# Linear attention feeding a gated MLP: zero products ahead of the first load, k loaded first, other buffers at the attention's end, and one head pair of the first batch divided on the chip

## The chip, the cores and the metric

The kernel runs on one core of a Trainium2 chip. The metric is device time in microseconds of one launch. Three runs of the kernel before took 1244.53, 1247.38 and 1248.22 us; the median is 1247.38 us.

The core has engines that each work through their own instruction list in order: TensorE (matrix products; PE in the profile, its weight loads PEld), VectorE (DVE), ScalarE (ACT), GpSimd (POOL), and SyncE (SP), which here issues the transfers between DRAM and the on-chip memory. [...]

## The reference

Attention has 8 batches, 8 heads, 576 tokens and 64 columns a head; its result, read as 4608 tokens of 512 columns, goes through a gated MLP.

```python
def phi(x):                                        # 64 -> 256 features
    proj = np.einsum('bhsd,df->bhsf', x, w_phi)    # w_phi: 64 x 128
    proj = proj - np.max(np.abs(proj), axis=-1, keepdims=True)
    return np.concatenate([np.exp(proj), np.exp(-proj)], axis=-1)
q_p, k_p = phi(q), phi(k)
kv  = einsum('bhsf,bhsd->bhfd', k_p, v);  z = sum(k_p, axis=2)
num = einsum('bhsf,bhfd->bhsd', q_p, kv)
den = einsum('bhsf,bhf->bhs', q_p, z)[..., None] + 1e-06
x = (num / den).transpose(0, 2, 1, 3).reshape(4608, 512)
out = ((x @ w_a) * (x @ w_b)) @ w_out              # 512 -> 1536 -> 512
```

Everything is float32. The weights of the MLP are float64 values handed over as 64-bit words, which the kernel decodes.

## The kernel before

**Attention** goes through 32 units, each a pair of heads of one batch. For one unit the k side loads k and v, forms the projection of k (tile `pk`, line 233, with the doubled weight matrix `wk32`), takes the largest absolute value on DVE (L247), subtracts it (L248), forms both exponentials on ACT (L256, L257) and accumulates `kvps` (L299). v carries a column of ones, so that row 64 of the result is the sum z. `k_finish` transposes that. The q side (`q_side`, one call per head) projects q (`pq`, L357), copies it (`p32`, L358), finds the maximum over partitions on POOL (`mb`, L361), subtracts it (L362), takes exponentials (L365, L366), multiplies with kv (`pn`, L381) and copies the 65 rows to `xn` (L382): 64 rows of numerators and one of denominators. `xn` has one buffer. Then `den` and `xun` are written to DRAM (L383, L384).

**The division** is done per pair by `reciprocals` (L392 on), through DRAM: the two denominator rows are read back in 128 partitions of 9 (`r`, L397), get eps and a reciprocal (L399, L400), are written (`rec`, L402), the numerators are read (`x32`, L404), the reciprocals are read broadcast over 64 partitions (`rb`, L407), multiplied (L409) and written as `xnorm` (L411). Each of these is one step of a generator.

**The MLP** runs in two passes over the hidden columns. Pass 0 has 12 blocks of 384 tokens (`moe_block`, products `pa` and `pb` at L609, outputs `po` at L632) and is interleaved with the attention; the first block needs only batch 0. Its x comes in four chunks of 128 columns, one from each head pair (`first_block_x`: `x_chunk` reads `xnorm` at L573, `x_make` splits it into two halves at L151 and L158). Pass 1 (`second_pass`, L696 and L744) comes after.

**Order.** Every generator's steps get a turn number (`attention_steps`): unit i starts at turn 5i for the first ones, a q side uses turns 0, 3, 4, 6 and 9 after that (3 later for the second head), the reciprocal steps of batch 0 the turns in `REC_TURNS0`, the x steps `X_TURNS`. The steps are traced in that order, and a planner that models time then orders each engine's list: work that it finds ready may be pulled ahead of work that is not, and loads go ahead as their buffers come free. `behind` keeps a reciprocal's transfers after the loads traced so far, and its DVE steps after the last traced subtraction L362.

**PSUM.** Up to the attention's end its products use four buffers with tag `att` (and one `kvacc`), the MLP three in `ps_moe`. Then the attention's pools close, and a pool `ps_late` with five buffers takes their banks; the last four blocks of pass 0 use it for `pa`, `pb` and `po`.

**Constants.** `attention_consts` loads w_phi twice on SP (L116), ahead of all other loads, and DVE builds from it, among others, the doubled matrix `wk32` (a memset at L122 and two copies at L125).

Of the kernel before, what the change touches and what calls it, by code (L numbers as in the profile page):

```python
# [10 lines left out]
F32 = mybir.dt.float32  # L11
# [3 lines left out]
ALU = mybir.AluOpType  # L15
# [17 lines left out]

REC_TURNS0, REC_TURNS, X_TURNS = (0, 1, 1, 1, 2, 2), (1, 3, 4, 5, 7, 8), (0, 1)
DECODE_TURN, BLOCK_LAG = 2, 1
PACE0, PACE, PACE0_UNTIL = 0.65, 0.75, 30


PLAIN_K, PLAIN_Q, PLAIN_KV, PLAIN_NUM = 9, 6, 11, 9

# [19 lines left out]
@with_exitstack  # L60
def tile_kernel(ctx, tc, qP, qD, km, kr, vm, vr, w_phi, w_a, w_b, w_out, out):

# [49 lines left out]

    def attention_consts(a1):
        w2 = a1.tile([P, F], F32, tag="rb", name="w2")
        for j in range(2):
            nc.sync.dma_start(w2[j * D : (j + 1) * D, :], w_phi)  # L116
        wh = a1.tile([P, F], F32R, name="wh")
        wl = a1.tile([P, F], F32R, name="wl")
        nc.vector.tensor_copy(wh, w2)
        nc.vector.tensor_tensor(wl, w2, wh, op=ALU.subtract)  # L120
        wk32 = a1.tile([P, 2, F], F32, tag="rk", name="wk32")
        nc.vector.memset(wk32, 0.0)  # L122
        for j in range(2):
            rows = slice(j * D, (j + 1) * D)
            nc.vector.tensor_copy(wk32[rows, j, :], w2[rows, :])  # L125
        wk2 = a1.tile([P, 2, F], F32R, name="wk2")
        nc.vector.memset(wk2.bitcast(F32), 0.0)
        nc.vector.tensor_copy(wk2[:, 0, :], wh)
        nc.vector.tensor_copy(wk2[:D, 1, :], wl[:D])
        ident = a1.tile([P, P], F32, name="ident")  # L130
        make_identity(nc, ident)
        rvz = []
        for i in range(2):
            t = a1.tile([P, 2, 2, D + 1], F32, name=f"rvz{i}")
            nc.vector.memset(t, 0.0)
            for r in range(2):
                nc.vector.memset(t[r * REST : (r + 1) * REST, r, :, D : D + 1], 1.0)
            rvz.append(t)
        vaug = []
        for i in range(2):  # L140
            t = a1.tile([P, NFULL, 2, D + 1], F32R, name=f"vaug{i}")
            nc.vector.memset(t[:, :, :, D : D + 1].bitcast(F32), 1.0)
            vaug.append(t)
        return w2, wh, wl, wk32, wk2, ident, rvz, vaug

# [186 lines left out]
    def q_side(b, pr, j, a1, a2, ps, consts, st):  # L332
# [41 lines left out]
        parts = [(s, kv_, e_) for kv_, e_ in products(st["kv", b, pr], es) for s in range(2)]  # L374
        xn = a2.tile([P, S], F32, tag="xn", bufs=1, name=f"xn_{u}")
        for i in range(2):
            tok = slice(i * HALF, (i + 1) * HALF)
            pn = ps.tile([P, 512], F32, tag="att", name=f"pn_{u}_{i}")
            for n_, (s, kv_, e_) in enumerate(parts):
                at = dict(start=(n_ == 0), stop=(n_ == len(parts) - 1))  # L380
                nc.tensor.matmul(pn[: D + 1, :HALF], kv_[:, 2 * j + s, :], e_[:, s, tok], **at)  # L381
            nc.scalar.copy(xn[: D + 1, tok], pn[: D + 1, :HALF])  # L382
        nc.sync.dma_start(den[b][h : h + 1], xn[D : D + 1])  # L383
        nc.sync.dma_start(xun[b][pr * P : (pr + 1) * P].rearrange("(d h) s -> d h s", h=2)[:, j], xn[:D])  # L384
        yield

# [27 lines left out]
    def attention_steps(pools, consts, st):  # L414
# [3 lines left out]
        def plan(unit, turns):  # L418
            for t in turns:
                stages.append((t, len(stages), unit))  # L420

        for i in range(B * NPAIR):
# [13 lines left out]
            rec_turns = REC_TURNS if b else REC_TURNS0  # L436
            plan(reciprocals(b, pr, pools[0]), [t0 + Q_STEP + Q_TURNS[-1] + t for t in rec_turns])
            if b == 0:
                plan(x_first, [t0 + Q_STEP + Q_TURNS[-1] + rec_turns[-1] + t for t in X_TURNS])
            if pr == NPAIR - 1:  # L440
                plan(b, [t0 + Q_STEP + Q_TURNS[-1] + rec_turns[-1]])
        stages.sort(key=lambda x: x[:2])
# [139 lines left out]
    def first_block_x():  # L582

        for c in range(NCC):
            x32 = x_chunk(0, 0, c, xpool, 2)
            yield
            x_make(0, 0, c, x32, xpool)
            yield

    def moe_block(p, j):  # L590
# [8 lines left out]
        for f in range(NFS[p]):  # L599
            u = f"{p}_{j}_{f}"  # L600
            pab = {}
            for nm in ("a", "b"):
                acc = psum.tile([P, T], F32, tag="moe", name=f"p{nm}_{u}")
                hi, lo = weights[(p, f, nm)]
                k = 0
                for cc in range(NCC):
                    xh, xl = xs[cc]
                    for w, x in ((hi, xh), (hi, xl), (lo, xh)):
                        nc.tensor.matmul(acc, w[:, cc * P : (cc + 1) * P], x, start=(k == 0), stop=(k == 3 * NCC - 1))  # L609
                        k += 1  # L610
                pab[nm] = acc
# [186 lines left out]

    away = {}
    weights, pools_moe, xpools, block_x, blocks, marks, loads = {}, [ps_moe], [xpool], {}, [0], [], []  # L800
    with ExitStack() as c:
        pools = attention_pools(c)
        consts = attention_consts(pools[0])
        work, tasks, due, st = deque(), {}, 0.0, {}
# [109 lines left out]
```

## Time and profile before

| What | Value |
|---|---|
| Median of three runs | 1247.38 us |
| The profiled execution | 1247.68 us |
| Its span | 1245.9 us |
| PE busy | 1212.7 us (97%) |
| DVE, ACT, POOL busy | 883.4, 726.5, 152.8 us |
| Mean granted PE clock | 0.993 |

The profile is of one execution, 1.8 us longer than its span, since something lies before the first and after the last instruction. The span's start is zero in every view. A timeline row is: start, duration, engine, line, operation, output<-inputs, shapes, count; in brackets how long that engine stood idle just before, and what released it. A row of the chain of waits is: start, duration, what the end of the program was waiting for then. A row of the table by stretches gives, for each stretch of time, the busy time of each engine with its number of instructions, the granted PE clock, the busy share of the DMA engines and the rate. One product of float32 operands makes two records on PE.

### The profile page before, as it was taken

The numbers are of one execution on the slowest core, as the hardware profiler recorded it, in microseconds if no ns is written. First come the engines' busy times: TensorE is split into PE (matmuls) and PEld (weight loads), VectorE is DVE, ScalarE is ACT, GpSimd is POOL, SyncE is SP. The second block draws the span as 40 slices with busy tenths as digits, with TensorE's granted clock in tenths as the row PEclk, the third lists the DMA queues.
The fourth block names the chain that finished last, engine by engine and source line by source line (L and its number), as shares of the span: only waits on it lengthen the run. The fifth ranks groups of instructions, "written<-read, shape, count | busy, mean of one in ns | idle before, by whom it ended". The sixth has DMA issues, their size and how long they took to land.

```text
span 1245.9 us, 20872 instructions
## 1 busy us (share of the span) xinstructions
PE 1212.7 (97%) x7724; PEld 1135.5 (91%) x7724; DVE 883.4 (71%) x1510; ACT 726.5 (58%) x1503; POOL 152.8 (12%) x70
## 2 busy tenths in 40 slices
PE   7898999999999999999999899999999999999998
PEld 5566888999999999999999899998999999999997
DVE  7967877988898988898887498655455455455443
ACT  5766777888878878878887355433232222222221
POOL 2331222122122121222122000000000000000000
PEclk9998999999999999999999999999999999999999
DMA  8776664554555454554443556982221231231121
GB/s 220 221 205 191 171 174 128 146 157 120 141 151 146 130 166 118 142 151 139 112 126 87 165 169 214 356 283 73 85 93 45 68 98 38 68 101 35 52 68 51
DMA packets 132101, 168.34 MB, mean 135 GB/s; under 512 B 41056, under 2 KB 77408, under 8 KB 132000
## 3 DMA queue, kind: packets, MB, share of 16 engines
q1 hardware_dynamic: 132000, 167.02, 45.5%
q8 instruction: 60, 0.98, 0.3%
q14 instruction: 41, 0.34, 0.1%
HBM read 119.49 MB, written 47.48 MB: 134 GB/s over the span
## 4 chain that ended last, share of the span: by engine, by line
PE 79%; DMA 10%; DVE 4%; ACT 3%; issue 2%; SPq 1%; POOL 0%; DVEq 0%; ACTq 0%
PE pab L696 20%; PE po L744 12%; PE pb L609 11%; PE pa L609 11%; PE po L632 9%; PE kvps L299 6%; PE pn L381 6%; PE pq L357 2%; PE pk L242 1%; DMA kept_wl_o<-wl_o 1%; DMA xnorm<-x 1%; DMA raw_a<-in_w_a 1%; DMA v<-in_vm 1%; DMA kept_wf_q_b_s<-wf_q_b_s 1%; DMA x<-xnorm 1%
## 5 line engine op out<-in xcount | busy, mean ns | idle before, releaser
L361 POOL PARTITION_ALL_REDUCE mb<-p x64 | 152.1, 2377 | 524.2 <-ACT p L358 416.1
L609 PE MATMUL pa<-xh,wh_a 128*128 128x384 f32 x288 | 100.0, 347 | 4.4 <-ACT xn L382 3.5
L151 ACT CAST hh<-h 128x384 fp32r<-128x384 f32 (+1 forms) x126 | 68.1, 560 | 59.7 <-DVE h L719 27.1
L609 PE MATMUL pa<-xl,wh_a 128*128 128x384 f32 x288 | 99.1, 344 | 0.0
L609 PE MATMUL pb<-xh,wh_b 128*128 128x384 f32 x288 | 98.8, 343 | 0.0
L609 PE MATMUL pa<-xh,wl_a 128*128 128x384 f32 x288 | 98.6, 342 | 0.0
L609 PE MATMUL pb<-xl,wh_b 128*128 128x384 f32 x288 | 98.3, 341 | 0.0
L609 PE MATMUL pb<-xh,wl_b 128*128 128x384 f32 x288 | 98.1, 341 | 0.0
L632 PE MATMUL po<-hl,wh_o 128*128 128x384 f32 x288 | 97.8, 341 | 0.0
L632 PE MATMUL po<-hh,wh_o 128*128 128x384 f32 x288 | 96.3, 342 | 0.7 <-ACT o L644 0.7
L632 PE MATMUL po<-hh,wl_o 128*128 128x384 f32 x288 | 97.0, 340 | 0.0
L158 DVE TENSOR_TENSOR hl<-h,hh 128x384 fp32r<-128x384 f32 (+1 forms) x126 | 76.0, 617 | 22.2 <-ACT hh L151 22.1
L158 DVE TENSOR_TENSOR qel<-qe,qeh 128x1152 fp32r<-128x1152 f32 x46 | 62.4, 1356 | 31.4 <-ACT qeh L151 29.2
L163 DVE TENSOR_TENSOR qs<-q,qs 64x576 fp32r<-64x576 f32 x52 | 63.4, 1220 | 25.0 <-ACT qs L151 22.5
L382 ACT COPY xn<-pn 65x288 f32<-65x288 f32 x128 | 48.9, 396 | 28.3 <-PE pn L381 16.6
L749 DVE TENSOR_TENSOR o<-po,o 128x512 f32<-128x512 f32 x36 | 24.1, 689 | 56.4 <-PE po L744 34.3
L609 PEld LDWEIGHTS pa<-xh,wh_a 128*128 128x128 f32 x288 | 54.7, 190 | 5.9 <-ACT xn L382 3.8
L256 ACT ACTIVATE ke<-kd 128x512 f32<-128x512 f32 x64 | 40.8, 637 | 29.4 <-DVE kd L248 28.9
L711 ACT COPY low<-pab 128x512 f32<-128x512 f32 x27 | 15.8, 586 | 71.3 <-PE pab L696 63.8
L744 PE MATMUL po<-hl,back_h 128*128 128x512 f32 x144 | 56.3, 391 | 0.0
L744 PE MATMUL po<-hh,back_l 128*128 128x512 f32 x144 | 56.2, 391 | 0.0
L632 PEld LDWEIGHTS po<-hh,wh_o 128*128 128x128 f32 x288 | 53.9, 188 | 1.6 <-ACT o L644 1.1
(268 smaller groups left out, 3843.2 us busy)
## 6 DMA issues: line engine op xcount, KB each, us to landing
q<-in_qD SPq DMA_DIRECT2D x52, 288.0 KB
k<-in_km SPq DMA_DIRECT2D x55, 256.0 KB
xun<-xn SPq DMA_DIRECT2D x64, 144.0 KB
x<-xun SPq DMA_DIRECT2D x32, 288.0 KB
rb<-rec SPq DMA_DIRECT2D x32, 288.0 KB
xnorm<-x SPq DMA_DIRECT2D x32, 288.0 KB
part<-o SPq DMA_DIRECT2D x48, 192.0 KB
o<-part SPq DMA_DIRECT2D x36, 256.0 KB
```

Of the source, the lines that this page charges most:

```text
L151: eng.copy(dst, src)
L158: eng_lo.tensor_tensor(lo, src, hi, op=ALU.subtract)
L163: eng_lo.tensor_tensor(hi_lo[D:], src[D:], hi_lo[D:], op=ALU.subtract)
L256: nc.scalar.activation(e[:, :, 0, :], d, AF.Exp)
L299: nc.tensor.matmul(st["kv_ps", b, pr][:width, j], v_[:, j, :width], e_[:, j], start=(left == NFULL and j == 0 and n_ == 0), stop=(left == ...
L361: nc.gpsimd.partition_all_reduce(mb, p32, P, bass_isa.ReduceOp.absmax)
L381: nc.tensor.matmul(pn[: D + 1, :HALF], kv_[:, 2 * j + s, :], e_[:, s, tok], **at)
L382: nc.scalar.copy(xn[: D + 1, tok], pn[: D + 1, :HALF])
L609: nc.tensor.matmul(acc, w[:, cc * P : (cc + 1) * P], x, start=(k == 0), stop=(k == 3 * NCC - 1))
L632: nc.tensor.matmul(accs[cc], w[:, cc * P : (cc + 1) * P], h, **at)
L696: nc.tensor.matmul(acc[to][:, i], w_, x_, skip_group_check=True, **at)
L744: nc.tensor.matmul(acc[cc], w[:, cc * P : (cc + 1) * P], h, **at)
```

## The change

Five things are done.

1. `w_two`, the doubled projection matrix with zeros (128x2x128), is prepared as an input and loaded straight into `wk32`; this load and the two of w_phi are issued from ACT instead of SP. So SP's first issue is k. The memset and copies at L122 and L125 go.
2. One half of `vaug` is set to zero by DVE, and five products of zeros, 192 columns wide, go to PE before everything else, into an `att` buffer that nothing reads.
3. Pair 3 of batch 0 (`DIRECT`) doesn't go through `reciprocals`. Its copy to `xn` adds eps to row 64 on the way (a bias column), and the new function `divide` takes the reciprocal of that one row of 576, spreads it over 64 partitions by a product with a row of ones, multiplies, and writes the chunk of the first block straight into its on-chip tile and all of x to `xnorm`.
4. The turns of batch 0 change: reciprocal steps from (0, 1, 1, 1, 2, 2) to (0, 2, 2, 3, 5, 5), x steps from (0, 1) to (1, 2) after them; for pair 3, (1, 2) after its last q step. The turn in which the first block is released stays the same.
5. The last head's `xn` uses the buffer `mb` instead of `xn`, and in every block of pass 0 the products of the first hidden slice use `ps_moe` instead of the late pool.

```diff
-REC_TURNS0, REC_TURNS, X_TURNS = (0, 1, 1, 1, 2, 2), (1, 3, 4, 5, 7, 8), (0, 1)
+REC_TURNS0, REC_TURNS, X_TURNS = (0, 2, 2, 3, 5, 5), (1, 3, 4, 5, 7, 8), (1, 2)
+WARM, WARM_TIMES = 192, 5
+DIRECT = (3,)
...
-    def attention_consts(a1):
+    def attention_consts(a1, ps):
+        wk32 = a1.tile([P, 2, F], F32, tag="rk", name="wk32")
+        nc.scalar.dma_start(wk32, w_two)
+        vaug = [a1.tile([P, NFULL, 2, D + 1], F32R, name=f"vaug{i}") for i in range(2)]
+        busy = vaug[1].rearrange("p c j d -> p (c j d)")[:, :WARM].bitcast(F32)
+        nc.vector.memset(busy, 0.0)
+        warm = ps.tile([P, WARM], F32, tag="att", name="warm")
+        for _ in range(WARM_TIMES):
+            nc.tensor.matmul(warm, busy[:, :P], busy, start=True, stop=True)
         w2 = a1.tile([P, F], F32, tag="rb", name="w2")
         for j in range(2):
-            nc.sync.dma_start(w2[j * D : (j + 1) * D, :], w_phi)
+            nc.scalar.dma_start(w2[j * D : (j + 1) * D, :], w_phi)
...
-        wk32 = a1.tile([P, 2, F], F32, tag="rk", name="wk32")
-        nc.vector.memset(wk32, 0.0)
-        for j in range(2):
-            rows = slice(j * D, (j + 1) * D)
-            nc.vector.tensor_copy(wk32[rows, j, :], w2[rows, :])
...
+        ones = a1.tile([P, 4 * (D + 1)], F32, tag="rvl", name="ones")
+        nc.vector.memset(ones[:, :D], 1.0)
+        eps = ones[: D + 1, D : D + 1]
+        nc.vector.memset(eps, 0.0)
+        nc.vector.memset(eps[D : D + 1], EPS)
...
-        xn = a2.tile([P, S], F32, tag="xn", bufs=1, name=f"xn_{u}")
+        direct = b * NPAIR + pr in DIRECT
+        xn = a2.tile([P, S], F32, tag="mb" if h + 1 == H and b + 1 == B else "xn", bufs=1, name=f"xn_{u}")
...
-            nc.scalar.copy(xn[: D + 1, tok], pn[: D + 1, :HALF])
+            if direct:
+                nc.scalar.activation(xn[: D + 1, tok], pn[: D + 1, :HALF], AF.Identity, bias=consts[7])
+            else:
+                nc.scalar.copy(xn[: D + 1, tok], pn[: D + 1, :HALF])
+        if direct:
+            yield from divide(b, pr, j, xn, ps, consts)
+            return
...
+    def divide(b, pr, j, xn, ps, consts):
+        u = f"{b}_{2 * pr + j}"
+        row = xn[D : D + 1]
+        nc.vector.reciprocal(row, row)
+        for i in range(2):
+            tok = slice(i * HALF, (i + 1) * HALF)
+            pr_ = ps.tile([P, 512], F32, tag="att", name=f"prec_{u}_{i}")
+            nc.tensor.matmul(pr_[:D, :HALF], consts[8][D : D + 1, :D], row[:, tok], start=True, stop=True)
+            nc.vector.tensor_tensor(xn[:D, tok], xn[:D, tok], pr_[:D, :HALF], op=ALU.mult)
+        if j == 0:
+            block_x32[pr] = xpool.tile([P, T1], F32, tag="x32", bufs=2, name=f"x32_0_0_{pr}")
+        nc.sync.dma_start(block_x32[pr].rearrange("(d h) s -> d h s", h=2)[:, j], xn[:D, :T1])
+        nc.sync.dma_start(xnorm[b][pr * P : (pr + 1) * P].rearrange("(d h) s -> d h s", h=2)[:, j], xn[:D])
+        yield
...
-            plan(reciprocals(b, pr, pools[0]), [t0 + Q_STEP + Q_TURNS[-1] + t for t in rec_turns])
+            if i not in DIRECT:
+                plan(reciprocals(b, pr, pools[0]),     [t0 + Q_STEP + Q_TURNS[-1] + t for t in rec_turns])
...
-            x32 = x_chunk(0, 0, c, xpool, 2)
+            x32 = block_x32.pop(c) if c in block_x32 else x_chunk(0, 0, c, xpool, 2)
...
-                acc = psum.tile([P, T], F32, tag="moe", name=f"p{nm}_{u}")
+                acc = (psum if f else ps_moe).tile([P, T], F32, tag="moe", name=f"p{nm}_{u}")
```

More of the change, by code (lines that the diff above doesn't have):

```diff
@@ L60, in tile_kernel @@
 @with_exitstack
-def tile_kernel(ctx, tc, qP, qD, km, kr, vm, vr, w_phi, w_a, w_b, w_out, out):
+def tile_kernel(ctx, tc, qP, qD, km, kr, vm, vr, w_phi, w_two, w_a, w_b, w_out, out):
     nc = tc.nc
@@ L138, in attention_consts @@
             rvz.append(t)
-        vaug = []
-        for i in range(2):
-            t = a1.tile([P, NFULL, 2, D + 1], F32R, name=f"vaug{i}")
+        for t in vaug:
             nc.vector.memset(t[:, :, :, D : D + 1].bitcast(F32), 1.0)
-            vaug.append(t)
-        return w2, wh, wl, wk32, wk2, ident, rvz, vaug
+        ones = a1.tile([P, 4 * (D + 1)], F32, tag="rvl", name="ones")
[3 more added lines that the diff above has]
+        nc.vector.memset(eps[D : D + 1], EPS)
+        return w2, wh, wl, wk32, wk2, ident, rvz, eps, ones, vaug
     def engine(step, b):
@@ L436, in attention_steps @@
             rec_turns = REC_TURNS if b else REC_TURNS0
-            plan(reciprocals(b, pr, pools[0]), [t0 + Q_STEP + Q_TURNS[-1] + t for t in rec_turns])
+            if i not in DIRECT:
+                plan(reciprocals(b, pr, pools[0]),     [t0 + Q_STEP + Q_TURNS[-1] + t for t in rec_turns])
             if b == 0:
-                plan(x_first, [t0 + Q_STEP + Q_TURNS[-1] + rec_turns[-1] + t for t in X_TURNS])
+                plan(x_first, [t0 + Q_STEP + Q_TURNS[-1] + (0 if i in DIRECT else rec_turns[-1]) + t for t in X_TURNS])
             if pr == NPAIR - 1:
-                plan(b, [t0 + Q_STEP + Q_TURNS[-1] + rec_turns[-1]])
+                plan(b, [t0 + Q_STEP + Q_TURNS[-1] + (X_TURNS[-1] if i in DIRECT else rec_turns[-1])])
         stages.sort(key=lambda x: x[:2])
@@ L799, in tile_kernel @@
     away = {}
+    block_x32 = {}
     weights, pools_moe, xpools, block_x, blocks, marks, loads = {}, [ps_moe], [xpool], {}, [0], [], []
@@ L802, in tile_kernel @@
         pools = attention_pools(c)
-        consts = attention_consts(pools[0])
+        consts = attention_consts(pools[0], pools[2])
         work, tasks, due, st = deque(), {}, 0.0, {}
@@ L898 @@
     vr = vr.reshape(B, H // 4, 2 * (S - n), 2, 2, D)
+    w_two = np.zeros((2, D, 2, w_phi.shape[1]), w_phi.dtype)
+    for j in range(2):
+        w_two[j, :, j] = w_phi
+    w_two = w_two.reshape(2 * D, 2, -1)
     arrays = {
-        "qP": qP, "qD": qD, "km": km, "kr": kr, "vm": vm, "vr": vr, "w_phi": np.ascontiguousarray(w_phi),
+        "qP": qP, "qD": qD, "km": km, "kr": kr, "vm": vm, "vr": vr, "w_phi": np.ascontiguousarray(w_phi), "w_two": w_two,
         "w_a": turned(moe_w_a).view(np.int64), "w_b": turned(moe_w_b).view(np.int64), "w_out": moe_w_out.view(np.int64),
```

## The prediction

> **What bounds the kernel now.** I read the engine totals first, then the table by stretches, and then the timeline and the chain of waits where that table shows PE idle.
>
> ```profile
> span 1245.9 us, 20872 instructions
> ...
> PE 1212.7 (97%) x7724; PEld 1135.5 (91%) x7724; DVE 883.4 (71%) x1510; ACT 726.5 (58%) x1503; POOL 152.8 (12%) x70
> ```
>
> PE is busy for all but 33.2 us (1245.9 - 1212.7). A change that leaves PE's work as it is can win at most these 33 us, and what busy time is lost to a low clock. So the question is which of the idle time each edit touches.
>
> ```profile
> 0.00:10.00 10.00, 4.89 (x12) 3.88 (x13) 4.92 (x22) 2.43 (x3) 0.68 (x6) 1.00 0.68 171
> 10.00:20.00 10.00, 8.64 (x39) 5.98 (x37) 6.09 (x13) 6.15 (x14) 2.38 (x2) 1.00 1.09 279
> 20.00:30.00 10.00, 8.01 (x38) 5.23 (x39) 9.83 (x17) 7.92 (x18) 4.29 (x2) 1.00 0.72 199
> ...
> 90.00:100.00 10.00, 7.27 (x32) 4.87 (x31) 4.63 (x10) 3.35 (x8) 2.14 (x1) 0.91 0.42 127
> 100.00:110.00 10.00, 8.41 (x27) 5.17 (x28) 8.26 (x17) 6.84 (x16) 2.50 (x1) 0.57 0.77 222
> ...
> 695.00:700.00 5.00, 2.52 (x17) 1.84 (x15) 2.12 (x2) 0.93 (x2) 0.00 (x0) 1.00 0.41 128
> 700.00:705.00 5.00, 3.33 (x12) 3.32 (x13) 0.28 (x2) 0.69 (x2) 0.00 (x0) 0.74 0.31 93
> ...
> 800.00:810.00 10.00, 10.00 (x58) 10.00 (x57) 8.40 (x19) 5.72 (x13) 0.00 (x0) 1.00 1.04 384
> ...
> 830.00:840.00 10.00, 9.54 (x79) 9.33 (x78) 8.35 (x19) 2.79 (x7) 0.00 (x0) 1.00 0.78 227
> 840.00:850.00 10.00, 8.68 (x62) 8.01 (x61) 6.88 (x15) 4.50 (x10) 0.00 (x0) 1.00 0.57 185
> ```
>
> The columns are PE, PEld, DVE, ACT and POOL busy, then clock, DMA share and GB/s. Three places lie under the edits. The start has 5.1 us idle in the first 10 us. The first block's wait at 90 to 110 has 2.73 + 1.59 = 4.3 us idle, and a clock of 0.91 and 0.57. The attention's end at 695 to 705 has 2.48 + 1.67 = 4.15 us idle and a clock of 0.74. These are the three terms of the sum.
>
> **The start (loads, zero products).**
>
> ```profile
> 0.72 1.22 SPq L116 DMA_DIRECT2D w<-in_w_phi  x2
> 1.99 0.58 SPq L172 DMA_DIRECT2D k<-in_km  x1
> 5.11 3.75 PE L233 MATMUL pk<-wk,k 128*128 128x256 f32 x8 [5.11 <-DMA k<-in_km]
> 18.84 0.76 DVE L362 TENSOR_TENSOR p<-p,mb 128x576 f32<-128x576 f32 x1 [1.88 <-POOL mb L361]
> 113.55 1.89 PE L299 MATMUL kvps<-ke,v 128*65 128x256 f32 x8
> ```
>
> ```profile
> 1.37 2.21 DMA w<-in_w_phi
> 6.27 6.20 DMA raw_a<-in_w_a
> ```
>
> The first two fences are from the timeline and the chain of waits. PE's first product waits for k, issued at 1.99 behind the two w_phi loads. With these off SP, k is issued at 0.72, 1.27 us sooner, and lands by 5.11 - 1.27 = 3.84. `wk32` now arrives by a 128 KB load issued from ACT near 0.7. No row has that size: the 32 KB one took 2.21 us, the 512 KB one 6.20 us in a crowd, so it lands between 2.9 and 6.9; I take about 4, nearer to the small one. In the bad end the first product is 1.8 us later than now.
>
> The eight records of 256 columns at 5.11 take 3.75 us, where the same width later takes 1.89: PE starts at half speed, whatever the clock column says. Five zero products are ten records of 192 columns, at the slow rate 10 x (192/256) x 3.75/8 = 3.5 us. They wait only for one small memset, so they run from about 1.1 to 4.6, and k finds PE free at 4.6 instead of 5.11. If PE is by then at full speed, the first eight records end at 4.6 + 1.9 = 6.5 instead of 8.86, a gain of 2.3; if not, 0.5. All eight slow records lasted 3.75 us, so 3.5 us of zeros should nearly do. [...]
>
> How much is passed on? The first DVE subtraction on the q side still stands at 18.84 behind POOL, whose first reduction no edit touches, and from 20 us on DVE is the full engine (9.83 of 10). DMA is full in 10 to 20 (1.09). So of 0.5 to 2.3 I book 1.0, with bounds from a loss of 1.8 to a gain of 2.3. The DVE work taken out (a memset, two copies) and put in (four small memsets) lies in idle time: DVE is busy 4.92 of the first 10 us. If that cover were gone it would be under 1 us either way. The `vaug` memset waits for the zero products, with the reduction of the first `pk` behind it, which comes later in any case.
>
> **The first block's wait (division on the chip, turns).**
>
> ```profile
> 86.62 2.44 DMA r<-den
> ...
> 89.61 3.10 DMA rec<-r
> ...
> 92.76 3.60 DMA rb<-rec
> ...
> 97.17 2.08 DMA xnorm<-x
> 99.28 3.64 DMA x<-xnorm
> ```
>
> ```profile
> 82.28 0.39 ACT L382 COPY xn<-pn 65x288 f32<-65x288 f32 x1
> 88.11 0.51 ACT L151 CAST xh<-x 128x384 fp32r<-128x384 f32 x1 [1.82 <-DMA x<-xnorm]
> 89.16 0.17 DVE L399 TENSOR_SCALAR r<-r 128x9 f32<-128x9 f32 x1 [4.33 <-DMA r<-den]
> 96.39 0.76 DVE L409 TENSOR_TENSOR x<-x,rb 128x576 f32<-128x576 f32 x1 [5.12 <-DMA rb<-rec]
> 97.85 0.78 PE L233 MATMUL pk_r<-wk,rk 128*128 128x256 f32 x2 [2.22 <-issue]
> 102.94 0.51 ACT L151 CAST xh<-x 128x384 fp32r<-128x384 f32 x1 [1.28 <-DMA x<-xnorm]
> 106.58 2.85 PE L299 MATMUL kvps<-ke,v 128*65 128x256 f32 x8
> ```
>
> Pair 3's numerators are copied at 82.28, and its chunk is cast at 102.94: 20 us, five DRAM trips of 2.1 to 3.6 us each. Two of them stop DVE in its order, for 4.33 and 5.12 us. Behind the second stands the subtraction L248 that frees a PSUM buffer, so PE's `pk_r` waits 2.22 us. After this gap the eight records of 256 columns take 2.85 us instead of 1.89: the clock has dropped. [...]
>
> Without this chain the idle 4.3 us go. The clock's cost is busy time times what is missing: 8.41 x 0.43 + 7.27 x 0.09 = 4.3 us. Together 8.6 us.
>
> What comes instead, for each of two heads: a reciprocal of a row of 576, two products of 64x288, two multiplications, two transfers. The nearest rows:
>
> ```profile
> L399 DVE TENSOR_SCALAR r<-r x32: 161/168/271, 42.1 to 704.7; 128x9 f32<-128x9 f32 x32
> ```
>
> ```profile
> L400 DVE RECIPROCAL r<-r x32: 201/206/217, 44.2 to 704.9; 128x9 f32<-128x9 f32 x32
> 76.57 2.10 PE L381 MATMUL pn<-qe,kvh 128*65 128x288 f32 x8
> ```
>
> Four products of 288 columns take 2.10 us, so the four new ones add 2.1 us to PE; nothing hides that. A multiplication of 576 takes 0.76 (L409). The reciprocal of 9 elements takes 0.206 us and the addition 0.168. If the 38 ns are only a longer pipe, 576 elements cost about what L409 costs, 0.76. If they are a price per element, it is 38/9 = 4.2 ns more, 0.76 + 2.4 = 3.2 us. If all 206 ns scale, 13.2 us. I take 0.8, since both 9-element rows are mostly a fixed cost. DVE has 4.33 + 5.12 = 9.45 us of waiting here to cover 2 x (0.8 + 0.8). So pair 3's chunk is ready at 82.7 + 0.8 + 1.1 + 0.8, plus a transfer. No row has one between two on-chip tiles; the DRAM ones above take 2.08 to 3.64 us, so that is 87.5 to 89 in place of 103.
>
> The other turns move pair 2's chain: its multiplication now stands behind one more subtraction L362, about 1 us, so its cast at 88.11 becomes about 89. Neither chunk then comes later than 95.6, where PE ran dry. The eps on the way is free, one copy for another; five transfers of SP's go and two stay as substitutes. `xn` is held longer, by a reciprocal, two products and two multiplications, some 3 us, under ACT's own idle time here (it works 3.35 of 10). If that is not cover enough, ACT's copies for pair 4 wait up to 3 us. The term is 8.6 - 2.1 = 6.5 us.
>
> **The attention's end (other buffers).**
>
> ```profile
> 695.76 0.48 ACT L644 COPY o<-po 128x384 f32<-128x384 f32 x1 [0.30 <-PE po L632]
> 700.93 0.69 ACT L382 COPY xn<-pn 65x288 f32<-65x288 f32 x2 [4.69 <-DMA xun<-xn]
> 701.67 0.44 PE L609 MATMUL pa<-xh,wh_a 128*128 128x384 f32 x1 [3.50 <-ACT xn L382]
> ```
>
> The last head's copy waits 4.69 us for the transfer that empties `xn`, and the next block's `pa` waits for that copy, since its PSUM bank is the attention's. `mb` is free by then, so the copy no longer waits; and `pa` no longer needs that bank: `ps_moe`'s last `po` was copied out at 695.76 + 0.48 = 696.24. PE's 3.50 us go, and with them the slow clock after them, 5 x (1 - 0.74) = 1.3 us. Later blocks have `ps_moe` standing free, at no cost. The term is 4.8 us; its bounds are 4.8 and 0, if another wait of the pool change takes over.
>
> **Sum.** 1.0 + 6.5 + 4.8 = 12.3 us, against the profiled execution: 1247.68 - 12.3 = 1235.4. The median of the runs is 0.3 lower, and I leave that inside the rounding: 1235.5 us. About 0.3%, 3.7 us, is what a measurement of this kernel can tell from no change.
>
> **The rivals.**
>
> *Slow reciprocal* (the other side). It sits in DVE's order, with the PE products and all of DVE's list behind it. At 3.2 us a row it adds 2 x 2.4 = 4.8, giving 1240; at 13.2 it adds 25 us, less at best the 9.45 of DVE's former waiting: 1251 to 1260. It turns the sign where 2 x (R - 0.8) eats 12.3 us, at R = 7 us or 12 ns an element. For it: the 206 against 168 ns. Against: at 4.2 ns an element more it stays far from 12. [...] Chance 0.10 that it costs over 2.4 us a row, half of that with a sign turned.
>
> *The late loads give it back.* After 800 the DMA engines are full (1.04) and PE idles 0.46 + 1.32 us at 830 to 850. If the loads that begin at the attention's end don't move with PE, the 4.8 us gained there come back as idle near 840: 1240.3. Against: up to 800 these loads are stepped by the blocks themselves, and their first issue hangs on the same last copy. Chance 0.15.
>
> *Pair 2 is late next.* If its chunk, two DRAM trips behind a later multiplication, comes 6 us after my 89, PE runs dry about as before, and half of the 6.5 is lost: 1238.7. For it: it has the turns moved back by three. Chance 0.10.
>
> *The zeros and the loads do nothing or harm*: 1236.4 to 1238.2, inside the forecast's own range, 1230 to 1238.5. The forecast has 0.60; 0.05 is left for a worse order by the planner, which I can't price, taken as losing most of the gain.
>
> The range is 1229.5 to 1243. Faster by over 0.3% holds the forecast, the milder slow reciprocal, and nearly all of the second and third rival, 0.89; within it, the planner's case and a remnant, 0.06; slower, the dear reciprocal, 0.05.
>
> **What would show it.** Right: the first `pk` near 4.6 with eight records in about 2 us; no DVE wait over 2 us between 80 and 105 and a clock of 1.00 there; `pa` within 0.5 us of the last `pn` near 690. Wrong: a RECIPROCAL row over 3 us; an `xh` cast after 97 that waits for `xnorm`; new idle at 820 to 850 of more than 1.8 us.

## The result and the profile after

The changed kernel takes 1257.65 us (median of four runs, 1252.54 to 1258.83) against 1246.24 us for the kernel before beside it. The ratio is 1.0079, 95% interval 1.0058 to 1.0099: slower, and outside the predicted range. A ratio here is an estimate from all the runs and not the quotient of the two medians, which is 1.0092. Two single slow runs further on, of 1291 us in e17 and 4219 us in e6, are left out of the ratios. The profiled execution took 1258.32 us. This page of the profile has its totals.

```profile
span 1256.5 us, 20911 instructions
...
PE 1219.1 (97%) x7742; PEld 1139.5 (91%) x7742; DVE 891.6 (71%) x1514; ACT 727.0 (58%) x1503; POOL 153.8 (12%) x70
```

PE is busy 6.4 us longer than before (1219.1 against 1212.7), about what the zero products and the products of the division take. It also idles 37.4 us instead of 33.2. So neither a gap nor busy time was saved on the whole. The table by stretches, with the columns of the one before, says where.

```profile
0.00:10.00 10.00, 7.97 (x29) 6.33 (x30) 4.73 (x24) 3.02 (x5) 0.68 (x6) 1.00 0.82 226
...
20.00:30.00 10.00, 7.77 (x26) 4.69 (x27) 9.79 (x17) 5.93 (x13) 4.50 (x2) 0.66 0.42 113
...
80.00:90.00 10.00, 8.03 (x37) 5.00 (x35) 6.99 (x9) 3.79 (x8) 0.34 (x1) 1.00 0.66 198
90.00:100.00 10.00, 6.80 (x21) 3.89 (x22) 6.54 (x7) 2.99 (x7) 1.80 (x1) 0.82 0.21 63
100.00:110.00 10.00, 10.00 (x41) 7.54 (x40) 5.31 (x11) 6.59 (x14) 2.14 (x1) 0.84 0.33 88
...
710.00:715.00 5.00, 1.71 (x9) 1.42 (x8) 1.78 (x3) 1.10 (x3) 0.00 (x0) 0.91 0.31 112
```

All three places still have their gap. From 20 to 30 us the clock is now 0.66. The first block's wait has moved from 90–110 to 80–100, with 5.2 us idle instead of 4.3, and a slow clock remains (0.82 and 0.84 where before has 0.91 and 0.57). The attention's end has 3.29 us idle in one piece. The timeline shows what stands in each place. First the start:

```profile
1.10 3.38 PE L123 MATMUL warm<-vaug 128*128 128x192 f32 x10 [1.10 <-DVE vaug L120]
4.53 1.99 PE L240 MATMUL pk<-wk,k 128*128 128x256 f32 x8
...
9.32 0.28 POOL masks.py:199 TENSOR_SCALAR_AFFINE_SELECT ident<-ident 128x128 f32<-128x128 f32 x1 [8.39 <-issue]
17.32 2.15 POOL L368 PARTITION_ALL_REDUCE mb<-p  x1 [7.72 <-issue]
...
22.23 0.67 PE L328 MATMUL pt<-ident,kvT 65*128 65x65 f32 x4 [4.71 <-ACT kvT L324]
22.69 6.28 PE L306 MATMUL kvps<-ke,v 128*65 128x256 f32 x16
```

The first products come as predicted (4.53, eight records in 1.99 us) and end 2.3 us ahead of before. POOL's first reduction does not come earlier: the five traces with the new start have it at 17.3 to 19.3 us, those with the old start and the identity matrix made on POOL at 15.1 to 18.9. PE runs dry at 22, for 4.71 us where before waited 2.93, and the sixteen records after the gap take 6.28 us instead of 2 x 1.89. Then the division:

```profile
79.23 3.74 DVE L405 RECIPROCAL xn<-xn 1x576 f32<-1x576 f32 x1
...
83.03 1.18 PE L409 MATMUL prec<-xn,ones 1*64 1x288 f32 x4 [1.21 <-DVE xn L405]
...
91.53 0.49 ACT L391 ACTIVATE xn<-pn,ones 65x288 f32<-65x288 f32 x1
...
92.05 3.74 DVE L405 RECIPROCAL xn<-xn 1x576 f32<-1x576 f32 x1 [3.43 <-ACT xn L391]
...
95.94 1.78 PE L409 MATMUL prec<-xn,ones 1*64 1x288 f32 x4 [2.10 <-DVE xn L405]
...
102.65 0.51 ACT L158 CAST xh<-x 128x384 fp32r<-128x384 f32 x1 [0.29 <-DMA x<-xn]
```

A reciprocal of one row takes 3.74 us, and PE, whose next product stands directly behind it, waits. The second head's numerators are complete only at 92.02, and pair 3's chunk is cast at 102.65, where the kernel before had it at 102.94. Last, the attention's end:

```profile
702.94 0.34 PE L640 MATMUL pa<-xh,wh_a 128*128 128x384 f32 x1
...
711.36 0.76 DVE L439 TENSOR_TENSOR x<-x,rb 128x576 f32<-128x576 f32 x1 [3.10 <-DMA rb<-rec]
712.03 0.55 DVE L645 TENSOR_TENSOR h<-pb,h 128x384 f32<-128x384 f32 x1
712.62 0.51 ACT L158 CAST hh<-h 128x384 fp32r<-128x384 f32 x1 [5.30 <-DVE h L645]
713.03 0.68 ACT L393 COPY xn<-pn 65x288 f32<-65x288 f32 x2
713.77 0.45 PE L640 MATMUL pa<-xh,wh_a 128*128 128x384 f32 x1 [3.29 <-ACT xn L393]
```

The copy no longer waits for its own buffer. It now stands on ACT behind a cast of a block, which waits for DVE's multiplication, which stands behind another that waits for `rb` from DRAM. And `pa` still waits for the copy: the block's first hidden slice, which has the experts' own pool, ran at 702.94 to 708.9, and the `pa` at 713.77 belongs to the second slice, whose pool still takes the attention's banks.

**A measure for where time is lost.** PE does the same products in all kernels, in somewhat different orders. For each trace I added up the work that PE had been given by each moment, without the zero products and those of the division. Each record counts with what it takes where nothing disturbs it, which the trace of before shows, from start to start, within 0.003 us: 0.216 us for 256 columns of the plain float32 products of the attention's first units and 0.243 for 288; in the later products 0.119, 0.132, 0.175 and 0.230 for 256, 288, 384 and 512 columns; 0.060 for a small transpose. A mere count of columns would shift the values by up to 2 us where orders differ, since a column of the early products takes nearly twice as long. The lag is the time at which a kernel has given PE as much as before had at the stated time, minus that time (us; negative is ahead). The times 210 and 690 lie clear of before's own gaps, near 199 and 700 us. A number in this table comes from the profiled execution alone.

| Kernel | 30 | 70 | 120 | 210 | 500 | 690 | 720 | 860 | 1200 |
|---|---|---|---|---|---|---|---|---|---|
| after | 2.9 | 5.3 | 7.7 | 9.3 | 10.4 | 9.0 | 7.9 | 8.5 | 8.5 |
| e1_start | 3.2 | 4.0 | 1.2 | 1.0 | 1.8 | 1.6 | 1.3 | -0.5 | -0.5 |
| e2_direct | -0.3 | -0.6 | 3.8 | 5.4 | 10.8 | 9.6 | 6.8 | 10.0 | 10.0 |
| e3_end | 1.3 | 1.4 | 1.1 | -0.4 | 0.9 | 1.3 | -4.3 | -6.4 | -6.4 |
| e4_copy | 4.0 | 7.3 | 2.7 | 5.8 | 7.0 | 5.6 | 5.0 | 5.5 | 5.5 |
| e9_turns | 3.1 | 1.9 | -1.9 | -4.9 | -3.6 | -4.2 | -5.5 | -4.0 | -4.0 |
| e11_mb | 1.1 | 0.5 | -1.0 | -0.9 | -0.7 | -0.2 | -4.8 | -3.9 | -3.9 |
| e12_later | 0.4 | 1.7 | -1.8 | -0.3 | 4.4 | 3.2 | 0.5 | 8.0 | 8.0 |
| e13_ready | 3.0 | 1.9 | -0.2 | 4.2 | 5.2 | 4.4 | 4.7 | 5.6 | 5.6 |
| e14_ready_mb | -0.3 | -0.9 | -1.9 | 2.6 | 3.7 | 3.2 | -1.4 | 1.8 | 1.8 |
| e15_turns_mb | 0.6 | -0.2 | -3.2 | -6.1 | -5.6 | -6.5 | -11.0 | -10.1 | -10.1 |
| e17_ready_only | 0.8 | -1.0 | -0.9 | -3.5 | -2.2 | -3.0 | -4.2 | -4.4 | -4.4 |
| e18_ready5 | 0.0 | 0.9 | -1.1 | 3.3 | 4.6 | 5.6 | 4.6 | 3.4 | 3.4 |

After loses 5.3 us by 70, 2.4 more by 120 and 1.6 more by 210, and gets 0.8 back from there to 1200. Its span is 10.6 us longer than before's; the other 2.1 us lie behind the last product. Of the 5.3, some 3 us can be chance: at 30 us the kernels with the old start lie anywhere from -0.3 to 3.1.

### The profile page after: what moved, and what is told of

It reads as the page before. It is cut to its first block, busy times and chain, and to the rows that moved or that the text cites. A ratio compares the mean times of both kernels' runs of the same rounds, so it can differ in the third digit from the quotient of the medians.

```text
span 1256.5 us, 20911 instructions
## 1 busy us (share of the span) xinstructions
PE 1219.1 (97%) x7742; PEld 1139.5 (91%) x7742; DVE 891.6 (71%) x1514; ACT 727.0 (58%) x1503; POOL 153.8 (12%) x70
## 4 chain that ended last, share of the span: by engine, by line
PE 70%; DVE 10%; DMA 9%; ACT 6%; issue 3%; SPq 1%; POOL 0%; DVEq 0%; ACTq 0%
PE pab L727 19%; PE po L775 11%; PE pa L640 10%; PE pb L640 9%; PE po L663 8%; PE kvps L306 5%; PE pn L389 5%; PE pq L364 2%; DVE qs L170 1%; DMA raw_a<-in_w_a 1%; PE pk L249 1%; DMA rb<-rec 1%; DMA r<-den 1%; DMA rec<-r 1%; DMA den<-xn 1%
## 5 line engine op out<-in xcount | busy, mean ns | idle before, releaser
L165 DVE TENSOR_TENSOR hl<-h,hh 128x384 fp32r<-128x384 f32 (+1 forms) x126 | 75.5, 614 | 22.9 <-ACT hh L158 22.8
L365 ACT COPY p<-pq 128x288 f32<-128x288 f32 x128 | 46.9, 400 | 17.6 <-PE pq L364 17.4
L165 DVE TENSOR_TENSOR xtl<-xs,xth 128x1024 fp32r<-128x1024 f32 x18 | 22.0, 1221 | 48.5 <-ACT xth L158 48.5
```

Source lines behind the costliest of these rows:

```text
L165: eng_lo.tensor_tensor(lo, src, hi, op=ALU.subtract)
L365: nc.scalar.copy(p32[:, tok], pq[:, :HALF])
```

## The experiments

Ratios are to the kernel before on the same chip, with 95% intervals. "Division" below means the division of pair 3 on the chip with its turns, "end" both buffers of the attention's end, "mb" the first of the two.

### The three parts alone

**e1_start**: before with the start alone (`w_two`, loads on ACT, zero products).

> The kernel before with the start alone changed (doubled matrix loaded, k first, zero products). Theory S: the first products end about 2 us sooner, but GpSimd's first reduction starts no sooner (17.32 us after the change, 16.65 before), so TensorE only waits longer ahead of it and the clock drops: 0 to 4 us slower than before. Theory P (the prediction's first term): 1 us faster, at most 2.3.

Measured 1249.33 us against 1249.14, ratio 1.0008 (0.9991 to 1.0024): nothing gained.

```profile
18.97 2.15 POOL L362 PARTITION_ALL_REDUCE mb<-p  x1 [9.72 <-issue]
...
23.89 0.66 PE L322 MATMUL pt<-ident,kvT 65*128 65x65 f32 x4 [6.26 <-ACT kvT L318]
```

PE waits 6.26 us where before waited 2.93. The lag of 4.0 at 70 us falls to 1.2 at 120: the first block's wait takes it up.

**e2_direct**: before with the division alone.

```diff
+ if i not in DIRECT:
      plan(reciprocals(...))     # and divide(), REC_TURNS0, X_TURNS as in the change
```

> The kernel before with the division on the chip and the new turns alone. Theory R: the reciprocal of one row of 576 takes 3.74 us, twice, holds VectorE's list and TensorE behind it, and this part alone makes most of the loss: 5 to 10 us slower than before. Theory S (the start makes the loss): this part alone is 2 to 7 us faster.

Measured 1257.37 us, ratio 1.008 (1.0054 to 1.0106). This part alone loses as much as all of them together.

**e3_end**: before with the end alone.

```diff
- xn = a2.tile([P, S], F32, tag="xn", ...)
+ xn = a2.tile([P, S], F32, tag="mb" if h + 1 == H and b + 1 == B else "xn", ...)
- acc = psum.tile([P, T], F32, tag="moe", ...)
+ acc = (psum if f else ps_moe).tile([P, T], F32, tag="moe", ...)
```

> The kernel before with the two other buffers at the attention's end alone. The prediction's third term: 4.8 us faster, no gap of TensorE near 698 us. Theory W: the last head's copies stand behind the next block's casts in ScalarE's order, which wait through VectorE for a pair's reciprocals from DRAM; the gap of 3.3 us stays and the time is within 1.5 us of before.

Measured 1241.41 us, ratio 0.9953 (0.9932 to 0.9974), faster than both kernels. The lag falls by 5.6 us between 690 and 720, near the 4.8 of the prediction, and by 2.1 more up to 860. In this trace, too, a `pa` waits for the last copy, at 703.16, but for 0.31 us only: ACT makes the copy at 702.24 and the block's cast after it, at 703.55.

### What in the division costs

**e4_copy**: after, with the reciprocal left out and a copy in its place, so that this pair's x is numerator times denominator.

```diff
- nc.vector.reciprocal(row, row)
+ nc.vector.tensor_copy(row, row)
```

> The changed kernel with a copy of the row of denominators in place of its reciprocal (it leaves out the reciprocal of pair 3 of batch 0, so that pair's x is numerator times denominator). Theory R: a copy takes about 0.7 us instead of 3.74, VectorE gets 6 us back and TensorE's two waits ahead of the spreading products go: 6 to 12 us faster than the changed kernel, at or under the time before. Theory S: within 3 us of the changed kernel.

Measured 1251.09 us, ratio 1.0025 (1.0006 to 1.0043), some 6.6 us less than after.

```profile
81.28 0.45 DVE L405 COPY xn<-xn 1x576 f32<-1x576 f32 x1
...
92.02 1.18 PE L409 MATMUL prec<-xn,ones 1*64 1x288 f32 x4 [0.85 <-DVE xn L405]
```

A copy of the same row takes 0.45. Between 70 and 120 us this kernel gains 4.6 us on before (7.3 to 2.7), after loses 2.4. The difference to after is within theory R's 6 to 12 us, but the time is not at or under that of before. The planner's lists also differ from after's between 79 and 203 us, so not all of the 6.6 us need be the reciprocal. And pair 3's chunk is cast at 101.55 even here: with the reciprocal gone, it still comes only 1.4 us before its old place.

**e8_spread**: after, with the denominators turned by nine small products to 64 partitions of 9 for the reciprocal, and spread back through a diagonal. All is computed.

```diff
- nc.vector.reciprocal(row, row)
+ for c in range(n): nc.tensor.matmul(pt_[:D, c : c + 1], cols[:, c], ones, ...)
+ nc.vector.reciprocal(r9[:D], pt_[:D, :n])
+ nc.vector.tensor_tensor(diag, ident_bcast, r9_bcast, op=ALU.mult)
```

> The changed kernel, with the row of denominators turned by nine small products into 64 partitions of 9 before its reciprocal, and spread again by a product of ones with a diagonal of the reciprocals: everything is computed. Theory R: VectorE spends about 0.2 + 0.75 us a head instead of 3.74, so it comes to the time with the mere copy, 1249 to 1253. Rival (the chain over ScalarE, VectorE and TensorE costs, not the reciprocal): 1255 or more.

Measured 1266.21 us, ratio 1.0146 (1.0129 to 1.0163).

```profile
83.34 0.21 DVE L411 RECIPROCAL r<-pden 64x9 f32<-64x9 f32 x1 [1.44 <-PE pden L409]
89.83 0.75 DVE L413 TENSOR_TENSOR diag<-ident,r 64x576 f32<-64x576 f32 x1 [2.18 <-DMA xnorm<-x]
90.64 2.18 PE L422 MATMUL prec<-diag,ones 64*64 64x288 f32 x4 [5.30 <-DVE diag L413]
```

The reciprocal is down to 0.21 us, and PE waits 5.30 all the same: the diagonal's multiplication comes 6 us behind the reciprocal on DVE, and waits last for a transfer out of the buffer (`x32`) that it shares. In this form the short reciprocal does not help; the chain with another buffer was not run.

**e12_later**: the division, with its products issued a turn after the reciprocal.

```diff
  nc.vector.reciprocal(row, row)
+ yield
- plan(q_side(...), [... for t in Q_TURNS])
+ plan(q_side(...), [... for t in (*Q_TURNS, Q_TURNS[-1] + 1)[: 5 + (i in DIRECT)]])
```

> The division on the chip with the new turns, start and end as before (1257.4 us, ratio 1.008), and its stage cut in two: the reciprocal is issued in one turn, and the products with the multiplications in the next, so that other products stand between pn and prec on PE. Theory P (PE's wait directly behind each reciprocal, and the slow clock after it, is the loss): the waits of PE at prec fall under 1 us, and the ratio falls to 1.003 or less. Theory D (DVE's own 7.5 us are the loss, whoever waits at once: DVE is the full engine up to 95 us, and all that stands behind it comes later): prec no longer waits, but other products wait for DVE instead, the subtraction's lag at 91 us stays at 10 us or more, and the ratio stays at 1.006 or more.

Measured 1255.69 us, ratio 1.0061 (1.004 to 1.0083).

```profile
79.89 1.18 PE L410 MATMUL prec<-xn,ones 1*64 1x288 f32 x4 [0.35 <-DVE xn L405]
...
86.49 0.50 ACT L391 ACTIVATE xn<-pn,ones 65x288 f32<-65x288 f32 x1 [0.36 <-DMA xnorm<-xn]
...
93.80 1.18 PE L410 MATMUL prec<-xn,ones 1*64 1x288 f32 x4
...
99.22 0.51 ACT L158 CAST xh<-x 128x384 fp32r<-128x384 f32 x1 [2.36 <-DMA x<-xn]
```

```profile
80.00:90.00 10.00, 10.00 (x47) 7.41 (x47) 5.94 (x12) 5.00 (x11) 2.14 (x1) 1.00 0.67 195
90.00:100.00 10.00, 9.11 (x41) 5.41 (x40) 5.88 (x7) 3.45 (x8) 2.14 (x1) 1.00 0.35 95
100.00:110.00 10.00, 10.00 (x52) 8.21 (x52) 9.51 (x18) 8.89 (x21) 2.14 (x1) 1.00 0.52 150
```

The timeline and the table by stretches show it: PE's waits at `prec` are gone, PE is idle 0.9 us from 80 to 110, the clock is 1.00, and the lag goes from 1.7 at 70 us to -1.8 at 120. That wait of the first block is gone, as predicted, but not because the chunk comes early: it is cast at 99.22. The time is hardly better: 1.5 us are lost up to 210, 4.7 up to 500, and 4.8 between 690 and 860. Theory P held for the place and failed for the total.

### The turns and the planner's order

**e9_turns** and **e10_old_turns**: before with the new turns alone, and the division with the old ones.

```diff
- REC_TURNS0, REC_TURNS, X_TURNS = (0, 1, 1, 1, 2, 2), ..., (0, 1)
+ REC_TURNS0, REC_TURNS, X_TURNS = (0, 2, 2, 3, 5, 5), ..., (1, 2)
```

> The kernel before with the later turns alone (REC_TURNS0 and X_TURNS); the division stays in DRAM for all pairs, and start and end are as before. Theory R (the loss of the division is its two reciprocals of 3.74 us, and what waits for them): the turns alone cost little, and the ratio lies in 0.998 to 1.003 (within 4 us of the kernel before). Theory T (the later turns are the loss: the chains of pairs 0 to 2 end later, and the first block starts later with pair 3 behind them): pair 3's chunk, already cast last at 103, comes some 2 to 4 us later still, and the ratio is 1.004 or more. Note that pair 3's chain is also moved by these turns here, so that T is given its best case.

> The division on the chip with the turns of before, and start and end as before. With the new turns it was 1257.4 us against 1247.4, a ratio of 1.008. Theory R: no more than 2 us better, ratio 1.006 to 1.009; both RECIPROCAL rows are at 3.74 us and PE waits 1.2 to 3.5 us at each of the products behind them. Theory T: without the later turns the loss shrinks to 1.003 or less.

The turns alone gave 1241.69 us, ratio 0.996 (0.9945 to 0.9974): a gain that neither theory had. The division with old turns gave 1258.76, 1.0092 (1.007 to 1.0114). So the turns help, if anything, and the division costs some 11 us with the old turns (e10 against before) and some 15 with the new ones (e2 against e9).

```profile
90.00:100.00 10.00, 9.29 (x48) 6.98 (x46) 5.67 (x12) 6.23 (x13) 2.73 (x2) 1.00 0.61 172
100.00:110.00 10.00, 7.65 (x29) 5.47 (x30) 4.55 (x9) 5.98 (x15) 2.14 (x1) 0.83 0.60 163
```

This is e9 where the first block waits: 3.06 us idle and a clock of 1.00 and 0.83, where before has 4.3 us, 0.91 and 0.57. From 70 to 120 us e9 gains 3.8 us on before, and e15, with the same turns, 3.0. The division gains 4.6 there with a copy for the reciprocal (e4) and 3.5 with the products a turn later (e12). So the turns alone win nearly as much at this wait as all of the division's work. Another 3.0 us come from 120 to 210: before's own gap at 199 is 1.39 us and followed by a clock of 0.83, e9's is 0.62 and the clock stays at 1.00.

I then counted, in the order of PE's products, how many expert products (`pa`, `pb`, `po`) stand ahead of each q-side projection. In after, e2, e4 and e12 this order is one and the same from about 270 us to the attention's end, with 4 to 30 more ahead than before. The planner has written another order far from the edit. In e9 it is that of before from about 320 us on, with 5 to 28 fewer ahead at most points between 130 and 180 us.

**e13_ready** and **e18_ready5**: e12_later, with batch 0's blocks given to the plan two and three turns later.

```diff
- plan(b, [... + (X_TURNS[-1] if i in DIRECT else rec_turns[-1])])
+ plan(b, [... + (4 if i in DIRECT else rec_turns[-1])])        # e18: 5
```

> The division on the chip with its products a turn later (e12_later: 1255.7 us, ratio 1.006), and batch 0's blocks given to the plan two turns later (4 for 2). From the 27th half-head's q-side products on, the number of expert products that PE has in its order ahead of each of these is then the same as in the kernel before; in e12_later it is 4 to 30 more at nearly all points up to the attention's end. Theory O (the loss after 110 us is this other order): the growth of the lag between 140 and 500 us falls from 8 us to under 2, and the ratio to 0.996 to 1.001. Theory D (the division's own work is the loss): ratio 1.004 or more, with the same waits at about 199 and 375 us.

> As e13_ready (division on the chip, products a turn later), with batch 0's blocks in the plan one turn later still (5 for 4). In e13 the expert products ahead of the attention's were still 19 to 30 more than before at the five points between about 100 and 200 us, and 25 at the last of them; here the last is 1 more than before. After 300 us they are within some 15 to 20 of before on both sides. Theory O: the lag's growth between 140 and 200 us falls from 7.7 us to under 4, and the ratio to 0.997 to 1.002. Theory D (the division's own work and transfers): the same growth, 1.002 or more.

e13 took 1252.1 us, ratio 1.0018 (1.0001 to 1.0036), e18 1251.7, 1.0029 (1.0015 to 1.0044). With the order of before restored after about 320 us, e13's lag grows by 1.4 us from 210 us to the end, where e12's grows by 8.3. So the other order costs e12 that much. But it has no fixed price: after, e2 and e4 have it too, and their lag changes by -0.8, 4.6 and -0.3 over the same stretch. (After and e4 also have the end's buffers, which take 6.0 from e3's lag there.) The growth between 120 and 210 us does not go with the order: it is 4.4 us in e13 and 4.4 in e18, whose surplus of products at the end of that stretch is gone, and 1.5 to 3.1 in after, e2, e4 and e12. Theory O failed there. In e18's timeline:

```profile
194.46 0.17 DVE L430 TENSOR_SCALAR r<-r 128x9 f32<-128x9 f32 x1 [3.85 <-DMA r<-den]
...
200.93 0.45 PE L641 MATMUL pa<-xh,wh_a 128*128 128x384 f32 x1 [3.26 <-ACT xh L158]
```

and in that of before:

```profile
189.28 0.17 DVE L399 TENSOR_SCALAR r<-r 128x9 f32<-128x9 f32 x1 [1.14 <-DMA r<-den]
```

DVE waits 3.85 us for the denominators of a later pair, still through DRAM, and PE runs dry soon after. In e2, e12 and after the same wait, near 191 to 203 us, is 2.4 to 3.3 us long. But e13 does not have it: its growth lies in several PE waits of 0.9 to 1.4 us between 146 and 205, for ACT and DVE. So one late transfer is not the whole of it, and what makes the kernels with the division lose 1.5 to 4.5 us between 120 and 210 us stays open.

**e17_ready_only**: before with batch 0's blocks three turns later and nothing else.

> The kernel before, with nothing changed but the turn at which batch 0's expert blocks enter the plan: three turns later, as in e9_turns, and the stages of the division in DRAM at their old turns. Theory O (the gain of the later turns, ratio 0.996, is that the expert products stand later against the attention's): 0.994 to 0.998. Theory C (the gain comes from the chains of pairs 0 to 3 standing elsewhere in DVE's order): 0.999 to 1.002.

Measured 1246.87 us, ratio 0.999 (0.9975 to 1.0005), a value of theory C, but its runs scatter from 1243 to 1251, and the profiled one was 4.4 us ahead. Nor do these two kernels separate the theories. The planner has given e17 nearly the lists of e9: on PE, DVE and ACT they differ in one exchange of neighbours each, at 87 to 97 us. From 120 to 210 us e17 gains 2.6 us as e9 gains 3.0; what it lacks is e9's gain of 3.8 between 70 and 120, around that exchange, where the transfers of pair 3 also stand elsewhere. Two runs on different chips, whose intervals meet (e9 ends at 0.9974), don't prove more, so the cause of the 5 us of e9 stays open; only their places are seen.

### Start and end, and what adds

**e5_start_ident**: e1, with the identity matrix loaded instead of made on POOL.

```diff
- make_identity(nc, ident)
+ nc.scalar.dma_start(ident, eye)
```

> The start alone, and the identity matrix loaded from DRAM instead of being made on GpSimd. Theory S: GpSimd's first reduction stood some 8 to 10 us behind that making, whatever TensorE did; now it starts near 10 to 12 us, the first subtraction follows, and the run is 2 to 6 us faster than with the start alone (1249.3). Rival: GpSimd's first reduction has its own start-up and stays near 17 to 19 us; within 1.5 us of the start alone.

```profile
10.51 2.14 POOL L362 PARTITION_ALL_REDUCE mb<-p  x1 [10.08 <-ACT p L359]
...
18.96 0.46 PE L322 MATMUL pt<-ident,kvT 65*128 65x65 f32 x4 [0.87 <-ACT kvT L318]
```

POOL's first reduction moves from 18.97 to 10.51 and PE's gap from 6.26 to 0.87: POOL's start is what held the start back. The time, 1247.39 us, ratio 0.9996 (0.9977 to 1.0016), shows no gain that can be told from none.

**e6_start_end** and **e7_direct_end**: start with end, and division with end.

> Start and end, without the division on the chip and with the old turns. Theory A (the parts add): the end part's 7.7 us of gain stay, 1241 to 1242. Theory B (the end part gains only where the planner happens to put the last copies ahead of the next block's casts): another start shuffles that order, and the time is anywhere between 1241 and 1250, with the gap of TensorE at the attention's end back when it is above 1246.

> Division on the chip, new turns and the end's buffers, with the old start. Theory A (the parts add): 8.2 us lost and 7.7 won, 1249 to 1251. Theory B: with the division the attention ends later against the blocks, the last copies stand behind a cast that waits for the last pair's reciprocals, and the end part wins nothing: 1255 to 1259, with a gap of about 3 us ahead of pa.

e6: 1249.03 us, 1.0002 (0.9977 to 1.0028); e7: 1255.3, 1.0058 (1.0041 to 1.0075). In e6's trace the end's gap is gone, but the time isn't kept, and its runs scatter widely (1240 to 1255). In e7 the gap is back, 3.1 us at 715. By their medians the parts do not add.

**e11_mb** and **e14_ready_mb**: before with mb alone, and e13 with mb.

> The kernel before with half of the end's edit: only the last head's numerators go to mb, while the accumulators pa and pb keep the attention's PSUM pool. Both halves together gave a ratio of 0.9953 (about -6 us). Theory B1 (my own prediction's reading: the copy's wait for xn is the whole wait, so that pa, whose bank that copy frees, comes early by itself): ratio 0.995 to 0.997, pa no more than 0.7 us behind the last pn's copies. Theory B2 (both edits are needed, since pa waits for a bank that only the copies free, and these stand behind other work on ACT): pa still waits 1.5 us or more, ratio 0.998 to 1.001.

> As e13_ready, with the last head's numerators in mb, which alone gave a ratio of 0.9975 (-3 to -4 us) in an unchanged order. Theory O: the attention's end is reached in the order of before, so that this part gives its 3 to 4 us again: 0.993 to 0.998. Theory N (what one part gains at the attention's end does not add to the others): the same as e13_ready within 1.5 us.

e11: 1244.62 us, 0.9975 (0.9961 to 0.9989), with an unchanged order on PE, DVE, ACT and POOL.

```profile
697.50 0.87 ACT L382 COPY xn<-pn 65x288 f32<-65x288 f32 x2 [1.49 <-PE pn L381]
698.42 0.45 PE L609 MATMUL pa<-xh,wh_a 128*128 128x384 f32 x1 [0.48 <-ACT xn L382]
```

The copy comes at once and `pa` waits 0.48 instead of 3.50, as theory B1 had it. e14: 1248.42 us, 0.9989 (0.9974 to 1.0004), 3.7 us less than e13, with 4.6 us gained between 690 and 720. So the end's gain returns to a kernel with the division once the order there is that of before.

**e15_turns_mb** and **e16_turns_end**: before with the new turns, and mb or the whole end.

> The kernel before with the later turns and mb, no division, old start. Alone they gave ratios of 0.996 and 0.9975. If they add: 0.9935 (about 1239 to 1240 us), and faster than both kernels. If the changed order takes the end's gain: 0.996 as the turns alone.

> As e15_turns_mb, with pa and pb of the first weight block in the experts' own PSUM pool as well. Both halves of the end alone gave 0.9953. If all add: 0.991 to 0.992 (1236 to 1238 us). If the end is worth the same as mb alone once the order differs: 0.9935; if nothing adds: 0.9955.

1237.97 us, ratio 0.9912 (0.9889 to 0.9935), and 1238.18, 0.9915 (0.9887 to 0.9944). Turns and mb add, and both versions beat before by about 11 us and after by about 20. The second PSUM choice adds nothing to mb here.

## Why the prediction was wrong

The sum asked for 12.3 us less, and the span of the profiled execution is 10.6 us longer. Of these 22.9 us, 6.3 lie ahead of 70 us, 8.9 between 70 and 120, 1.6 between 120 and 210, 4.0 from there to 1200 (4.8 booked, 0.8 won) and 2.1 behind the last product.

**The start (booked 1.0, none seen).** The first products came at 4.53 in 1.99 us, as worked out. The step that failed is "how much is passed on": the 2.3 us were lost again at POOL's first reduction, and with interest, since PE then idled longer and was slowed after it (16 records in 6.28 us). The prediction had named that reduction as untouched, and yet booked 1.0. With e1's interval a gain of 1.0 us (0.9992) is just possible.

**The first block's wait (booked 6.5).** This term failed, in its cost and in its path. The cost is the reciprocal, taken as 0.8 and measured at 3.74. The prediction had 3.2 for a price per element, and set it aside since "both 9-element rows are mostly a fixed cost". By an estimate from the two rows, 0.206 us for 128x9 and 3.74 for 1x576, the price is 6.2 ns an element of the row on top of 0.15 us: mostly a fixed cost at 9 elements, but not at 576. The cover named for it, DVE's 9.45 us of former waiting, was no cover: the product stood directly behind the reciprocal in PE's order, so that PE paid too, with waits of 1.21 and 2.10 us.

The path is the chunk of pair 3, forecast for 87.5 to 89 instead of 103. It was cast at 102.65 in after, at 98.17 in e2, 99.22 in e12, and at 101.55 with a mere copy in e4; with the turns alone, through DRAM, at 101.78. The prediction counted from the copy at 82.28. But the two heads of the pair share the one `xn`, and the first holds it until its result has been read out. "Some 3 us, under ACT's own idle time" was this hold, charged to pair 4, and it fell on pair 3 itself: its last copy began at 91.53 in after, 91.00 in e4, 88.92 in e12 and 88.54 in e2. In e12, and by 0.35 us in e2, the second head's first copy waits for the transfer `xnorm<-xn` of the first; in after and e4 its row names no such wait. From the last copy's end to the cast the chain then took 9.2 to 10.6 us instead of 4.8 to 6.3. In e4 the multiplication begins 3.9 us after the product, and the cast comes 4.65 us after the transfer's issue; in after the transfer is issued 1.8 us after the multiplication. So that the wait shrank at all (4.6 us in e4, 3.5 in e12) doesn't show the predicted cause: the turns alone gained 3.8.

The rival *Slow reciprocal* had the cost, but priced a row of 3.7 us at about 1241, with the sign turned only from 7 us. It missed the PE waits behind it, the late chunk, and everything after 120 us.

**What was costed at nothing.** The planner's order was left at 0.05. The division alone makes it write another order from 270 to 700 us; e12 lost 8.3 us after 210 us with it and e13, without it, 1.4, but after itself, with it, lost nothing there, and only missed the end's gain. The stretch from 120 to 210 us had no price either; the kernels with the division lose 1.5 to 4.5 us there, 1.6 in after, and the cause is open. *Pair 2 is late next* came true in small: pair 2's chunk was cast at 92.47 instead of 89, and PE waited 0.95 us for it. The turns, costed at "about 1 us" of delay, gain 5 alone.

**The attention's end (booked 4.8).** About right alone: 5.6 us in e3, 4.6 in e11. In part this is luck: the slow clock was charged to the whole stretch (5 x 0.26 = 1.3), while the first block's term charged it to busy time, which here would give 0.9. In after the end gave nothing; the lower bound "0, if another wait of the pool change takes over" came true. The steps that failed are "so the copy no longer waits" and "`pa` no longer needs that bank". The first holds for the buffer but not for ACT's order, in which the copy now stood behind a cast that waited 5.30 us. The second holds for a block's first slice alone, and in after the waiting product was of the second. *The late loads give it back* did not happen in e3, whose idle time at 820 to 870 went from 1.8 us to nothing; in after 2.55 us stand at 850 to 860, but with nothing gained there to give back.

**The signs named beforehand.** Of the signs of being right only the first `pk` came. Of those of being wrong, the RECIPROCAL row over 3 us came. New idle of 2.55 us stands just behind the named stretch, at 850 to 860, in a kernel that is 8 us late. The pair's cast at 102.65 waits for the transfer from `xn` and not for `xnorm`, but stood only 0.3 us before its old place.

## What to carry over

Time a new instruction form in its own shape before booking it: the reciprocal of one partition of 576 took 3.74 us, that of 128 partitions of 9 took 0.21. Follow a buffer's holder through the new chain before calling its hold covered: the next one to want it may be the other half of the same chain. In a kernel whose order a planner writes, compare the orders first: an edit can rewrite engine lists half a millisecond away, two edits meant to differ can give nearly the same lists, and parts that gain alone may not add. And of two parts ordered in one list, look at what stands directly behind the slow one on another engine.

## What the runs showed of the hardware

A DVE reciprocal of 1x576 took 3.74 to 3.75 us in after, e2, e12, e13 and e18, a copy of the same row 0.45 us in e4, and a reciprocal of 128x9 (before) or 64x9 (e8) 0.21 us. POOL's first partition reduction began 7.72 us after the end of its affine select in after, 9.66 us in e3 and 9.72 us in e1, with nothing visible in between; in e5, where that operation is left out, it began at 10.51 us of the span, against 17.32, 17.95 and 18.97.

The trace of after has six PE gaps of 2 us and more, the first products aside. Behind four of them records soon stood at about half speed: 0.32 us apart for 384 columns behind the 3.29 us at 713.77, against 0.18 from 717.70, and 0.43 us apart for 256 columns, against 0.22, behind 4.71 us at 22.23, 2.29 at 61.49 and 2.10 at 95.94. Behind the other two they did not: 0.13 us apart for 288 columns behind 2.77 us at 210.12, and 0.12 for 256 behind 2.55 us at 855.91. Ahead of a product of the same form as at 210.12, a gap of 2.78 us in e12 was followed by records 0.24 us apart (from 199.27).
